# Loads of values, queries and first weights that wait for the start of a page of TensorE's program

## The chip, the cores and the metric

The kernel runs on one core of a Trainium2 chip. Its five engines run their own instruction streams: TensorE (PE in the profile; PEld are its weight loads), VectorE (DVE), ScalarE (ACT), GpSimd (POOL) and SyncE (SP). Here SyncE issues nearly all of the transfers between the chip's main memory and the on-chip buffers. The metric is the time of one execution in microseconds (us) of device time. [...]

## What is computed

A block-sparse attention layer feeds a mixture of experts with one expert per token. The attention has 4 batches, 8 heads, 768 positions and 64 values per head; positions are grouped in 24 blocks of 32.

```python
scores = scale * np.matmul(q, k.transpose(0, 1, 3, 2))
# kept: the blocks beside the diagonal, the first and last block of rows and of columns,
# and three sampled blocks for each block of queries; all others are set to -1e9
attn = softmax(scores)
x = np.matmul(attn, v)                      # as 3072 tokens of 512
...
do_compute = x @ w_skip > 0
e_idx = argmax(x @ w_gate)                  # one of 8 experts, 512 -> 1024 -> 512
out[do_compute] = x + gate * (relu(x @ w1[e]) @ w2[e])
```

## The kernel before, in words

The first and the last block of queries attend to all positions. They are worked first, by 16 units of the class `Dense`. The other 22 blocks of queries ("columns") each attend to at most eight blocks of keys: the first, the last, three near ones and three sampled ones. They are worked by 44 units of the class `Sparse`, two for each column, `b = 0` and `b = 2`, that is, two of the four batches each. `ORDER` takes the columns in turn from the lower and from the upper half (1, 12, 2, 13, ...), and each half has one store of keys (`kg`) and one of values (`va`, `vb`), so a store is refilled while the other half's column is worked.

A unit has these steps: `S` (16 score matmuls of PE, L452), `M` (maxima on DVE, L458), `X` (exponentials on ACT, L464), `T` (transposes on PE, L471), `V` (their copy by ACT, L477), `A` (32 matmuls with the values, L490) and `N` (division by the sums on DVE, L501 to L503, into `xs`). `sparse_step(k)` interleaves them by hand: `S` of unit k+2, `N` of unit k-1, `T` of unit k+1, `A` of unit k, then `M` and `X` of unit k+2, then `after` of unit k-1, which issues four stores of the finished column, and `fill`, which issues what is due by step number. In between come small pieces of routing (`work`). The whole program order is fixed when the kernel is built; `manual_schedule` keeps it.

The loads in question are issued by SyncE, in the order of the program:

- `load_v(i)`, called at the end of `A` of a column's second unit, for the next column of the same store. It loads one near block and three sampled blocks, 260 KB each, into the store that this `A` was the last to read. The numbers of the sampled blocks are read into three registers of SyncE between the first load and the others. The next `A` on this store is three units later.
- `load_q(i)`, called in `S` of a column's first unit: 512 KB of queries, for two columns at once, so in every second column. `load_k`, called in `S` of the second unit, has GpSimd copy the blocks of keys within the chip (L204, L223) and then scale the queries.
- `load_w`, called in `fill` in the last steps of the stage, two loads of 512 KB a step: the weights of the first expert, in four quarters each (`"1"`, then `"2"`). They go into `kts`, where the keys were. `split_w` then makes two parts of each piece: ACT writes `w1h` (L545), GpSimd `w1l` (L547).

Near the end of the stage two groups of early tokens are fetched (`xe`, L639) and transposed (L622), and their two parts written by ACT (`xeh`, L624) and DVE (`xel`, L625). Then the experts begin: matmuls from L878 on. `xs` has two buffers, so a column's `N` writes where the second column before it was stored from.

Of the kernel before, what the change touches and what calls it, by code (L numbers as in the profile page):

```python
# [20 lines left out]
NB, BS = 24, 32  # L21
# [3 lines left out]
N, DM, E, FF = 3072, 512, 8, 1024  # L25
# [8 lines left out]
LC = NC + 2  # L34
NEVER = float(E * LC * P * P)
VA = 8
NEAR = 8
KINDS = [1, 2, 4, 5, 6, 8, 9, 10, 11, 12]
HALF = NB // 2

ORDER = [i for pair in zip(range(1, HALF), range(HALF, NB - 1)) for i in pair]
# [5 lines left out]
def tile_kernel(ctx, tc, qs, qd, kt, v, sb, wg, w1, w2, out):  # L47
    nc = tc.nc
# [3 lines left out]
    vrows = v.rearrange("n s b h d -> n s (b h) d")  # L52
# [29 lines left out]
    def load_dense_k(u):  # L82
        b, pp = divmod(u, 4)
        if u == 0:
            qts[b] = dp.tile([P, 4, 64], F32, name="qt", bufs=3)
            nc.sync.dma_start(out=kts[:, 0, 0:384], in_=kt[0, :, 0, 0:384])
            nc.scalar.dma_start(out=qts[b][:, 0], in_=qd[b, :, 0])
            nc.sync.dma_start(out=kts[:, 0, 384:768], in_=kt[0, :, 0, 384:768])
            nc.scalar.dma_start(out=qts[b][:, 1:4], in_=qd[b, :, 1:4])
            return  # L90
        if pp == 0:
            qts[b] = dp.tile([P, 4, 64], F32, name="qt", bufs=3)
            nc.sync.dma_start(out=qts[b], in_=qd[b])
        nc.sync.dma_start(out=kts[:, u], in_=kt[b, :, pp])

    def load_dense_v(u):

        b, pp = divmod(u, 4)
        if u % 2 == 0:
            vts[u] = vts[u + 1] = dp.tile([P, 6, 4, VD], F32, name="vt", bufs=VA // 2)  # L100
        elif u > 1:
# [3 lines left out]

    for u in range(VA):
        load_dense_k(u)
# [92 lines left out]
    def vslot(x, z):  # L200
        return vslots[x][z // 4][z % 4]
# [4 lines left out]
    def store(i):  # L206
        return i // HALF

    def window(i):
        return (i - 1, i, i + 1) if i in ORDER[:2] else (i + 1,)  # L210

    def next_of(i):
        return i + 1 if i + 1 in ORDER and store(i + 1) == store(i) else None
# [16 lines left out]
    qt, qts2 = {}, {}  # L230

    def load_q(i):
        z = ORDER.index(i)
        if z % 2 == 0:
            qts2[z // 2] = ap.tile([P, 2, NPAIR, BS], F32, name="q")
            for n in range(2):
                qt[ORDER[z + n]] = qts2[z // 2][:, n]
            nc.sync.dma_start(out=qts2[z // 2], in_=qs[z // 2])

    def load_v(i):  # L240
        x = store(i)
        if i in ORDER[:2]:
            nc.sync.dma_start(out=vslot(x, 0), in_=vrows[0])
            nc.sync.dma_start(out=vslot(x, 1), in_=vrows[NB - 1])
        for blk in window(i):
            nc.sync.dma_start(out=vslot(x, 4 + blk % 3), in_=vrows[blk if 0 < blk < NB - 1 else NB])
        for vr, z in zip(blocks_of(mybir.EngineType.SP, vidx, i, NB), (2, 3, 7)):
            nc.sync.dma_start(out=vslot(x, z), in_=vrows[bass.ds(vr, 1)].rearrange("n s h d -> (n s) h d"))


    def route(xta, tiles):
# [186 lines left out]
    class Sparse:  # L438
# [6 lines left out]
        def S(self):  # L445
            self.sp = [ps_s.tile([P, 2, 256], F32, name=f"sp{w}") for w in range(2)]
            for g in range(2):
                for a in range(4):
                    p = 4 * (self.b + g) + a
                    for w in range(2):  # L450
                        ws = slice(64 * w, 64 * w + 64)
                        nc.tensor.matmul(out=self.sp[w][32 * a:32 * a + 32, g], lhsT=qt[self.i][ws, p, :], rhs=kg[self.x][ws, p, :].rearrange("p (k c j) -> p c k j", k=2, j=2), start=True, stop=True)  # L452
            if next_of(self.i):
                (load_k if self.b else load_q)(next_of(self.i))

        def M(self):
# [22 lines left out]
        def A(self):  # L479
            drain = self.i == NB - 2 and self.b == 2  # L480
            if drain:
                self.op = ps_s.tile([P, 512], F32, name="sp0")[:, 0:4 * VD].rearrange("p (g w d) -> p g w d", g=2, w=2)
            else:
                self.op = ps_o.tile([P, 2, 2, VD], F32, name="op")
            for g in range(2):
                for w in range(2):
                    for t in range(2):
                        vt = (va, vb)[t][self.x]
                        for a in range(4):
                            nc.tensor.matmul(out=self.op[32 * a:32 * a + 32, g, w, :], lhsT=self.pt[:, g, 2 * w + t, 32 * a:32 * a + 32],  # L490
                                             rhs=vt[:, 8 * (self.b + g) + 2 * a + w, :], start=(t == 0), stop=(t == 1))
            if self.b == 2 and next_of(self.i):
                load_v(next_of(self.i))

# [33 lines left out]
    raws = {}  # L528

    perm = rt.tile([1, E], I32, name="perm")  # L530
# [3 lines left out]
    def load_w(which, p, part=0, parts=1, place=None, er=None):  # L534

        n = 4096 * ((2 * p - (which == "1")) % 3 if place is None else place)
        raws[which, p] = kts.rearrange("p a s -> p (a s)")[:, n:n + 4096]
        sz = 4096 // parts
        cs = slice(sz * part, sz * part + sz)
        er = nc.sync.value_load(perm[0:1, p:p + 1], min_val=0, max_val=E - 1) if er is None else er  # L540
        nc.sync.dma_start(out=raws[which, p][:, cs], in_=(w1 if which == "1" else w2)[bass.ds(er, 1), :, cs].rearrange("o p c -> (o p) c"))

    def split(h, l, r, what, eng=None):
        if "h" in what:
# [130 lines left out]
    def mix(a, c):  # L675
        n = max(len(a), len(c))
        for z in range(n):
            for l in (a, c):
                if z < len(l):
                    l[z]()  # L680
# [37 lines left out]
    def fill(q):  # L718

        if q == 1:  # L720
            first.extend(setup())
        if 1 <= q <= 7:
            mix(first[4 * q - 4:4 * q], [])
        if 0 <= q and q + VA < 18:
            if q + VA < 16:
                load_dense_k(q + VA)
            load_dense_v(q + VA - 2)
        if q in (8, 10):
            i = ORDER[q // 2 - 4]
            load_q(i)  # L730
            load_v(i)
            load_k(i)
        if q == nd:
            den.close()
            wp = ctx.enter_context(tc.tile_pool(name="wp", bufs=1, side="right"))
            wt.update({"1" + t: wp.tile([P, 4096], F32R, name=f"w1{t}") for t in "hl"})
        z = q - nq + 10
        if -4 <= z < 4:
            load_w("12"[(z + 4) // 4], 0, z % 4, 4)
        if 3 <= z < 11:  # L740
            split_w("1", 0, z - 3, 8, "hl", nc.gpsimd)

# [106 lines left out]
    now = mc.tile([1, 2 * E], I32, name="now")  # L849
# [146 lines left out]
    def parts(p):  # L996

        def each(f):
            if NEAR <= f + 3 < NK2:
                split_w("1", p, f + 3, 8)  # L1000
# [155 lines left out]
    x = [mp.tile([P, NK1, CS * P], F32R, name=n, bufs=1) for n in ("xh", "xl")]  # L1156
# [114 lines left out]
```

## Time and profile before

| what | value |
| --- | --- |
| median of 3 runs | 491.8 us (489.98 to 494.74) |
| profiled execution | 492.82 us |
| its span, first to last instruction | 491.1 us |
| instructions in the span | 16939 |
| PE busy | 441.3 us |
| DVE busy | 321.2 us |
| ACT busy | 250.8 us |
| POOL busy | 149.3 us |
| granted clock of TensorE, mean | 0.97 |

The profile comes from one execution, and its times count from the first instruction. "Busy" is the time in which an engine works on an instruction; a matmul of 32-bit numbers is run as two passes, each with its own weight load. "Idle before" is the time in which an engine did nothing ahead of an instruction, with what ended it: another engine's instruction, a DMA, or "issue", where the profile shows no semaphore that it waited for. The DMA share is the mean busy share of 16 DMA engines.

### The profile page before, as it was taken

What the parts mean: (1) busy time and instruction counts of PE and PEld (TensorE: products, weight loads), DVE (VectorE), ACT (ScalarE), POOL (GpSimd) and SP (SyncE); (2) the same over time, 40 slices, a digit from 0 to 9 for tenths busy, and PEclk for the clock granted to TensorE, in tenths of its full rate; (3) what the DMA queues carried; (4) which work ended last, traced back from release to release, by engine and by line L of the source; (5) the groups of instructions that cost most, each with busy time, mean ns of one, the idle gap of its engine ahead of it and who ended that gap; (6) DMA issues with size and microseconds to landing.
All of it is one profiled execution on the core that took longest, in us unless ns stands there. A gap on an engine that the chain in (4) does not pass through costs nothing. (4 is left out here: it accounts for less than half of the span.)

```text
span 491.1 us, 16939 instructions
## 1 busy us (share of the span) xinstructions
PE 441.3 (90%) x6666; PEld 342.1 (70%) x6666; DVE 321.2 (65%) x838; ACT 250.8 (51%) x581; POOL 149.3 (30%) x198
## 2 busy tenths in 40 slices
PE   5989999889999999997499999899999894999994
PEld 1757777666667666655477789787878664878984
DVE  2878766956878776956565286664777776465621
ACT  2535586756766765667231264463435484343500
POOL 2004625433443433426604420403313142201002
PEclk9989999999999999999689999999999995999999
DMA  8998837765767765779328209383371949281001
GB/s 253 375 301 282 306 117 222 244 206 160 241 187 238 214 186 177 235 230 332 102 94 311 92 27 332 107 294 112 109 274 53 337 148 328 82 301 38 23 16 45
DMA packets 43824, 94.91 MB, mean 193 GB/s; under 512 B 7463, under 2 KB 27048, under 8 KB 40546
## 3 DMA queue, kind: packets, MB, share of 16 engines
q1 hardware_dynamic: 39808, 84.27, 51.8%
q0 software_dynamic: 3376, 8.09, 4.7%
q8 instruction: 74, 1.21, 1.0%
q14 instruction: 132, 1.08, 0.7%
q10 hardware_dynamic: 434, 0.26, 0.2%
HBM read 84.51 MB, written 10.88 MB: 194 GB/s over the span
## 5 line engine op out<-in xcount | busy, mean ns | idle before, releaser
L477 ACT COPY pt<-tp 128x512 f32<-128x512 f32 x88 | 52.3, 598 | 48.2 <-PE tp L471 48.2
L464 ACT ACTIVATE pr<-sp,m 128x256 f32<-128x256 f32 x176 | 69.0, 482 | 3.5 <-DVE m L458 3.2
L458 DVE TENSOR_REDUCE m<-sp 128x2 f32<-128x512 f32 x88 | 56.5, 684 | 18.5 <-PE sp L452 18.2
L878 PE MATMUL hp<-xh,w1h 128*128 128x256 f32 (+3 forms) x192 | 57.8, 301 | 2.5 <-PE yp L934 2.5
L880 PE MATMUL hp<-xh,w1l 128*128 128x256 f32 (+3 forms) x192 | 57.4, 299 | 0.0
L879 PE MATMUL hp<-xl,w1h 128*128 128x256 f32 (+3 forms) x192 | 57.4, 299 | 0.0
L883 ACT ACTIVATE hh<-hp 128x256 fp32r<-128x256 f32 (+2 forms) x56 | 21.3, 380 | 68.5 <-PE hp L880 53.3
L452 PE MATMUL sp<-kg,q 64*32 64x256 f32 x1408 | 53.9, 391 | 2.6 <-issue 2.4
L490 PE MATMUL op<-va,pt 128*32 128x65 f32 x1376 | 46.2, 223 | 6.5 <-issue 5.6
L471 PEld LDWEIGHTS tp<-ident,pr 128*128 128x128 f32 x352 | 37.6, 141 | 20.4 <-issue 7.4
L204 POOL COPY kg<-kts 128x512 f32<-128x512 f32 x30 | 19.4, 663 | 105.9 <-PE sp L452 68.6
L74 POOL DMA_INDIRECT out<-o,lt x17 | 17.0, 998 | 112.5 <-DVE o L949 107.6
L932 PE MATMUL yp<-w2h,hh 128*128 128x512 f32 x120 | 49.1, 409 | 1.9 <-DVE o L949 1.9
L471 PE MATMUL tp<-ident,pr 128*128 128x128 f32 x352 | 48.8, 280 | 0.8 <-ACT pt L477 0.7
L933 PE MATMUL yp<-w2l,hh 128*128 128x512 f32 x120 | 48.1, 400 | 0.3 <-issue 0.3
L934 PE MATMUL yp<-w2h,hl 128*128 128x512 f32 x120 | 47.8, 398 | 0.0
L547 DVE TENSOR_TENSOR w2l<-kts,w2h 128x512 fp32r<-128x512 f32 x64 | 43.5, 686 | 5.7 <-ACT w2h L545 3.3
L490 PE MATMUL op<-vb,pt 128*32 128x65 f32 x1376 | 44.3, 220 | 1.8 <-issue 1.7
L223 POOL COPY kg<-kts 128x512 f32 x66 | 42.1, 684 | 8.1 <-POOL kg L204 8.1
L490 PEld LDWEIGHTS op<-va,pt 128*32 128x32 f32 x1376 | 32.7, 109 | 15.3 <-issue 13.8
L886 DVE SCALAR_TENSOR_TENSOR hl<-hp,hh 128x256 fp32r<-128x256 f32 (+2 forms) x56 | 23.4, 417 | 30.3 <-ACT hf L885 12.7
L545 ACT CAST w2h<-kts 128x512 fp32r<-128x512 f32 x64 | 39.0, 619 | 1.8 <-DVE w1l L547 1.8
(221 smaller groups left out, 902.2 us busy)
## 6 DMA issues: line engine op xcount, KB each, us to landing
kts<-w SPq DMA_DIRECT2D x64, 512.0 KB, 6.3
va<-v SPq DMA_DIRECT2D x48, 260.0 KB, 3.9
vb<-v SPq DMA_DIRECT2D x48, 260.0 KB, 4.2
kts<-kt SPq DMA_DIRECT2D x15, 384.0 KB, 7.5
q<-qs SPq DMA_DIRECT2D x11, 512.0 KB, 5.4
out<-xs SPq DMA_DIRECT2D x88, 64.0 KB, 4.2
vt<-v SPq DMA_DIRECT2D x7, 780.0 KB, 8.7
vt<-v SPq DMA_DIRECT2D x2, 390.0 KB
```

The source lines that it names most:

```text
L452: nc.tensor.matmul(out=self.sp[w][32 * a:32 * a + 32, g], lhsT=qt[self.i][ws, p, :], rhs=kg[self.x][ws, p, :].rearrange("p (k c j) -> p c ...
L458: return [lambda w=w: nc.vector.tensor_reduce(out=self.mx[:, w], in_=self.sp[w], axis=AX.X, op=ALU.max, negate=True) for w in range(2)]
L464: nc.scalar.activation(out=self.pr[:, g, w], in_=self.sp[w][:, g], func=AF.Exp, bias=self.mx[:, w, g:g + 1])
L471: nc.tensor.transpose(out=tp[:, u, :], in_=self.pr[:, g, u // 2, (u % 2) * P:(u % 2) * P + P], identity=ident)
L477: nc.scalar.copy(out=self.pt[:, g], in_=self.tp[g])
L490: nc.tensor.matmul(out=self.op[32 * a:32 * a + 32, g, w, :], lhsT=self.pt[:, g, 2 * w + t, 32 * a:32 * a + 32], rhs=vt[:, 8 * (self.b + g) ...
L878: nc.tensor.matmul(out=hp[:, 0:w], lhsT=wh[:, f, k, :], rhs=xh[:, k, 0:w], start=(k == 0), stop=False)
L879: nc.tensor.matmul(out=hp[:, 0:w], lhsT=wh[:, f, k, :], rhs=xl[:, k, 0:w], start=False, stop=False)
L880: nc.tensor.matmul(out=hp[:, 0:w], lhsT=wl[:, f, k, :], rhs=xh[:, k, 0:w], start=False, stop=(k == NK1 - 1))
L932: nc.tensor.matmul(out=yp, lhsT=hh[:, f, cs], rhs=wh[:, f, :], start=(f == 0), stop=False)
L933: nc.tensor.matmul(out=yp, lhsT=hh[:, f, cs], rhs=wl[:, f, :], start=False, stop=False)
L934: nc.tensor.matmul(out=yp, lhsT=hl[:, f, cs], rhs=wh[:, f, :], start=False, stop=(f == NK2 - 1))
```

## The change

The kernel estimates, while it is built, how many instructions TensorE has run, and so where each page of 256 instructions begins. `size_of` counts a matmul as four instructions, a transpose as two; the term `done // 149` stands for others, and `PROLOGUE` for those ahead of the kernel. Loads of the three kinds are no longer issued where they are called: `paged` puts them on a list, sorted by size (260 for values, 512 for queries and weights). `page_check`, called in `S` and `A`, sees when a new page has begun and has `release` issue the smallest loads, up to 1600 KB together, each with a dependency on the instruction of TensorE that began the page. `release()` without an argument issues all that are left, without such a dependency; this is done in `S` of a column's second unit, ahead of `load_k`, and once in `fill`, at the step where the last two weight loads were issued. The loads for the first two columns stay as they were. The eight weight loads are put on the list together, at the step of the first of them, and share one register for the expert's number. The registers of the sampled blocks are still read in `load_v`.

```diff
+PAGE = 256
+PROLOGUE = 98
...
-            nc.sync.dma_start(out=qts2[z // 2], in_=qs[z // 2])
+            load = lambda: nc.sync.dma_start(out=qts2[z // 2], in_=qs[z // 2])
+            load() if i in ORDER[:2] else paged(512, load)
...
+    class Paged:
+        waiting, seen, done, page = [], 0, 0, None
+
+    def size_of(i):
+        if type(i) is mybir.InstLdweights:
+            return 1
+        if type(i) is mybir.InstMatmult:
+            return 1 if i.ldweights is False else 2 if i.is_transpose else 4
+        return 0
+
+    def paged(size, load):
+        Paged.waiting.append((size, load))
+        Paged.waiting.sort(key=lambda w: w[0])
+
+    def release(most=1 << 30, ins=None):
+        while Paged.waiting and most >= Paged.waiting[0][0]:
+            size, load = Paged.waiting.pop(0)
+            most -= size
+            dma = load()
+            if ins is not None:
+                tc.add_manual_dep(dma.ins, ins.name, mybir.DependencyInfo(mybir.DependencyClass.Sync, mybir.DependencyReason.DATA),
+                                  reason="behind the fetch of a page")
+
+    def page_check():
+        bb = nc.cur_bb.bb.instructions
+        for i in bb[Paged.seen:]:
+            Paged.done += size_of(i)
+            page = (Paged.done + Paged.done // 149 + PROLOGUE) // PAGE
+            if page != Paged.page and size_of(i):
+                Paged.page = page
+                release(1600, i)
+        Paged.seen = len(bb)
...
+        now = (lambda size, load: load()) if i in ORDER[:2] else paged
         for blk in window(i):
-            nc.sync.dma_start(out=vslot(x, 4 + blk % 3), in_=vrows[blk if 0 < blk < NB - 1 else NB])
+            now(260, lambda blk=blk: nc.sync.dma_start(out=vslot(x, 4 + blk % 3), in_=vrows[blk if 0 < blk < NB - 1 else NB]))
         for vr, z in zip(blocks_of(mybir.EngineType.SP, vidx, i, NB), (2, 3, 7)):
-            nc.sync.dma_start(out=vslot(x, z), in_=vrows[bass.ds(vr, 1)].rearrange("n s h d -> (n s) h d"))
+            now(260, lambda vr=vr, z=z: nc.sync.dma_start(out=vslot(x, z), in_=vrows[bass.ds(vr, 1)].rearrange("n s h d -> (n s) h d")))
...
+                    page_check()
             if next_of(self.i):
+                if self.b:
+                    release()
                 (load_k if self.b else load_q)(next_of(self.i))
...
+                        page_check()
...
-        if -4 <= z < 4:
-            load_w("12"[(z + 4) // 4], 0, z % 4, 4)
+        if z == -4:
+            er = nc.sync.value_load(perm[0:1, 0:1], min_val=0, max_val=E - 1)
+            for n in range(8):
+                paged(512, lambda n=n: load_w("12"[n // 4], 0, n % 4, 4, er=er))
+        if z == 3:
+            release()
```

## Rows read from the trace of the kernel before

**Rows 1.** Busy time of PE, and the queue of instructions, on the page.

```profile
PE 441.3 (90%) x6666; PEld 342.1 (70%) x6666; DVE 321.2 (65%) x838; ACT 250.8 (51%) x581; POOL 149.3 (30%) x198
...
q8 instruction: 74, 1.21, 1.0%
```

**Rows 2.** Windows: busy (count) of PE, PEld, DVE, ACT, POOL; clock, DMA share, GB/s.

```profile
61.40:86.00 24.60, 24.40 (x707) 17.47 (x708) 16.13 (x43) 18.43 (x44) 9.74 (x15) 1.00 0.55 169
86.00:110.00 24.00, 20.86 (x641) 15.03 (x639) 17.54 (x53) 15.21 (x38) 9.89 (x14) 1.00 0.73 224
```

**Rows 3.** Waits of PE from 61 to 211: total us, times, longest.

```profile
PE op L490 <- issue: 6.1, 8, 1.3
PE sp L452 <- issue: 2.4, 4, 0.8
```

**Rows 4.** Timeline of PE, three resumptions: start, us, what, idle before.

```profile
153.76 0.26 PE L490 MATMUL op<-va,pt 128*32 128x65 f32 x3 [0.57 <-issue]
...
176.86 0.25 PE L490 MATMUL op<-va,pt 128*32 128x65 f32 x2 [1.19 <-issue]
...
210.09 0.42 PE L342 MATMUL rps<-phi,lsb 128*128 128x48 f32 x2 [1.19 <-issue]
```

**Rows 5.** Windows of two pages, columns as in rows 2.

```profile
171.82:176.86 5.04, 3.85 (x128) 2.83 (x128) 3.72 (x15) 3.18 (x9) 2.27 (x4) 1.00 0.61 185
...
158.07:162.12 4.05, 4.05 (x127) 2.60 (x133) 2.39 (x8) 2.65 (x7) 2.35 (x4) 1.00 0.60 180
```

**Rows 6.** DMA at 174.4:174.5, 177.9:178.0, 155.2:155.3: packets, MB, share.

```profile
q8 instruction: 1, 0.02, 58.2%
...
q8 instruction: 1, 0.02, 65.5%
...
q8 instruction: 1, 0.02, 69.1%
```

**Rows 7.** Timeline of SyncE, value loads: start, us, issues.

```profile
154.23 0.49 SPq L246 DMA_DIRECT2D vb<-v  x1
155.63 1.14 SPq L248 DMA_DIRECT2D va<-v  x2
...
169.96 1.16 SPq L248 DMA_DIRECT2D va<-v  x2
```

**Rows 8.** Window from the start to a resumption, columns as in rows 2.

```profile
0.00:93.87 93.87, 84.75 (x1600) 58.68 (x1601) 65.22 (x216) 53.14 (x119) 29.04 (x60) 0.98 0.80 265
```

**Rows 9.** Instructions of L490, its events: ns min/median/max, first and last.

```profile
L490 PEldq EVENT_SEMAPHORE  x85: 51/51/747, 63.4 to 229.8; - x85
```

**Rows 10.** DMA issues from 61 to 232: count, KB each, median us to landing.

```profile
vb<-v SPq DMA_DIRECT2D x40, 260.0 KB, 4.2
...
q<-qs SPq DMA_DIRECT2D x9, 512.0 KB, 5.4
kts<-w SPq DMA_DIRECT2D x8, 512.0 KB, 6.3
```

**Rows 11.** Timeline of PE, first values used of one column.

```profile
164.25 0.32 PE L490 MATMUL op<-va,pt 128*32 128x65 f32 x8
```

**Rows 12.** Timeline of SyncE, last columns and weights.

```profile
220.46 0.51 SPq L246 DMA_DIRECT2D vb<-v  x1
...
226.46 3.28 SPq L511 DMA_DIRECT2D out<-xs  x4
```

**Rows 13.** Timelines of PE, DVE and POOL, last columns.

```profile
229.48 0.32 PE L490 MATMUL op<-va,pt 128*32 128x65 f32 x8 [0.91 <-DMA va<-v]
...
233.65 0.42 DVE L503 TENSOR_TENSOR xs<-op,rs 128x256 f32<-128x256 f32 x1 [2.30 <-DMA out<-xs]
...
235.53 0.66 PE L622 MATMUL rps<-ident,xe 128*128 128x128 f32 x4 [2.98 <-DVE xel L625]
...
228.37 6.21 POOL L547 TENSOR_TENSOR w1l<-kts,w1h 128x512 fp32r<-128x512 f32 x5 [3.52 <-ACT w1h L545]
```

**Rows 14.** Window of the half clock, columns as in rows 2.

```profile
236.00:249.80 13.80, 9.38 (x41) 7.04 (x40) 5.94 (x12) 3.56 (x8) 6.06 (x9) 0.51 0.14 34
```

More of the change, by code (lines that the diff above doesn't have):

```diff
@@ L540, in load_w @@
         er = nc.sync.value_load(perm[0:1, p:p + 1], min_val=0, max_val=E - 1) if er is None else er
-        nc.sync.dma_start(out=raws[which, p][:, cs], in_=(w1 if which == "1" else w2)[bass.ds(er, 1), :, cs].rearrange("o p c -> (o p) c"))
+        return nc.sync.dma_start(out=raws[which, p][:, cs], in_=(w1 if which == "1" else w2)[bass.ds(er, 1), :, cs].rearrange("o p c -> (o p) c"))
     def split(h, l, r, what, eng=None):
```

## The prediction

> **What bounds it now.** I read the busy times first: TensorE (PE) is busy 441.3 us, 90% of the span, and the queue of instructions, q8, brings 74 packets of together 1.21 MB, so 16 KB each [rows 1]. The change touches the sparse stage, from about 61 to 235 us, so I then read windows there. Between 61.4 and 86 PE is busy 24.4 of 24.6 us; between 86 and 110 only 20.9 of 24, while VectorE (DVE) is at 17.5 and GpSimd at 9.9 [rows 2]. PE sets the pace, and what keeps it from work is to be looked for in its waits.
>
> From 61 to 211 us they have one cause, "issue", which is no semaphore and no engine: 6.1 us before L490, 2.4 before L452 [rows 3] and 1.2 before L342 [rows 4], 9.7 us in 13 waits, none over 1.3. The timeline shows what they look like: PE stops in the middle of a run of equal matmuls and goes on with the same line, as at 153.76, 176.86 and 210.09 [rows 4]. Between two such resumptions, 171.82 and 176.86, lie 128 matmuls and 128 weight loads [rows 5]: 256 instructions, and 16 KB over 256 is 64 bytes each, so PE waits for a page of its own code.
>
> The packets show why. The page entered at 171.82, the resumption before, calls for the next; that packet starts between 174.4 and 174.5, 2.6 us later, takes 58.2% of 16 x 0.1 = 0.9 us, and PE goes on at 176.86, 1.4 us behind its end. The page entered at 176.86 has its packet just after 177.9, 1.1 us later [rows 6]. So
>
> stop = (entry to packet) + 1.0 + 1.4 - length of the page.
>
> With 1.1 that is a fetch of 3.5 us; a page that isn't stopped lasts 4.05 [rows 5], so there is about half a microsecond to spare for queueing. What stood in the queue at 171.82: the value loads issued from 169.96 to 171.1 [rows 7] among others; at 176.86 these were long down.
>
> **The loads go behind the fetch.** The mark in `page_check` must hit the right instruction. Up to the resumption at 93.87 the trace has 1600 + 1601 instructions of PE [rows 8]; 3201 + 3201 // 149 + 98 = 3320, 8 short of 13 x 256, a tenth of a microsecond, and the few bf16 matmuls of the ranks, which `size_of` counts as four where two run, close that. So the marks fit the program before. The new dependencies add signals to some 30 TensorE instructions. If each cost an event instruction of its own it would be 30 x 51 ns = 1.5 us [rows 9] and the marks would drift; I take 0, since a matmul can carry a signal (the bound is 1.5).
>
> The nearest row to a load behind the entry is the page entered at 153.76 [rows 4], with the first load issued at 154.23 [rows 7]: the packet that it called came just after 155.2 [rows 6], 1.5 us behind the entry, so 1.5 + 2.4 = 3.9 us, and PE has no stop before the page entered at 158.07 [rows 5], 4.3 us on. So the page in which a column's loads go out costs nothing. The page after it meets the tail: four loads of 260 KB, every second column 512 KB of queries, and four stores, which are not marked. The values of a column need 4 x 0.57 us to issue (two in 1.14 [rows 7]) and 4.2 to land [rows 10], so they are down some 6 us after the release; the next call comes after about 4.1, waits perhaps a microsecond, and its page just hides that. With queries there is one more issue, and 5.4 us to land [rows 10]: I put 0.4 us of stop on each of the 9 query loads, 3.6, with a rest about 4 us. So of 9.7 us I take 5.7 as gained. Bounds: 9.7 if no tail is met, 0 if each stop only moves one page on.
>
> [...]
>
> **The values come later.** The wait holds a column's loads by up to a page: those free at 154.23 [rows 7] wait for the page entered at 158.07 [rows 5], 3.8 us, and the mean is half a page, 2.1. Their user, the column's first `A`, starts at 164.25 [rows 11]. With 0.3 us for the signal, 3 x 0.57 to the last issue and 4.2 to land, these end at 164.3, just at the edge; the mean case ends 1.7 us early. Two things help: the register loads that now part the first load from the second (154.23 to 155.63 [rows 7]) are done ahead of the wait, and `release()` in `S` of the column's second unit bounds the delay. Since PE without stops gets to `A` sooner, I charge 0.1 us for some 5 of 20 columns near that edge, 0.5. Bounds: 0, and the slower rival below.
>
> **Queries, stores, scaling.** Queries are asked for two columns ahead, so a page and 5.4 us are hidden by the units between. GpSimd scales them behind its key copies and has room (9.9 of 24 us busy [rows 2]); were that cover gone, `S` would wait. Behind the waiting load on SyncE stand the stores of the finished column; their buffer is written again two columns later, so a page of delay costs nothing. I charge 0.
>
> **The last columns and the first weights.** Now SyncE issues two weight loads of 512 KB a step, and they hold back what follows: the last column's values go out from 220.46, and the stores of the column before from 226.46, with two more weight loads in between [rows 12]. The values stop PE 0.9 us at 229.48; for the stores DVE waits 2.3 us at 233.65, and through it PE 2.98 us at 235.53, with the second transpose of the early rows; then ScalarE, then GpSimd's last splits [rows 13]. After the change one weight load goes out with the values of column 11 at the page of 210.1 [rows 4], three at the next (a page is 4.1 us: 214.2), and at the one after, 218.3, the last column's values with the fifth weight load behind them. The last three go behind the stores. So the values leave 2 us and the stores some 4 us earlier: the 0.9 vanishes, and the transpose can follow its unit and the first `xel` at about 232.9, 2.6 us sooner. Then GpSimd's splits bound it: five took 6.21 us from 228.37 [rows 13], two more at that rate end at 237.1, where PE was still idle. I take 2.9 in all; bounds 0 and 0.9 + 3.0 = 3.9. The clock is at half level, 0.51, from 236 to 249.8, behind these idle times, with 9.4 us of PE's work in it [rows 14]. PE still idles for GpSimd and at the branch, so I leave that; if the clock stayed up, up to half of the 9.4 would be won, and this is why the low end is below the sum.
>
> **Sum.** The profiled execution took 492.8 us, its span 491.1 and 1.7 around it. 492.8 - 5.7 - 2.9 + 0.5 = 484.7. The median of the runs is 1.0 below the profiled one, which gives 483.7: forecast 484.
>
> **Rivals.**
> - All stops go: 492.8 - 9.7 - 2.9 - 1.0 = 479. For it: without the register loads a burst is shorter. Against: queries and stores in its tail. 0.14.
> - The stops move one page on, as the bytes are the same: some 8.5 of 9.7 us stay, 492.8 - 1.2 - 2.9 + 0.5 - 1.0 = 488. For it: DMA is busy 0.73 of the window that has the worst stops [rows 2]. 0.13.
> [...]
> - It doesn't do what it says: the marks drift off the pages, loads wait for nothing useful, and stops stay: 490 to 491. 0.05.
> - Slower: the values land too late for `A`. If the released bursts landed in the 6.3 us of the weight loads [rows 10] in place of 4.2, the column of 164.25 would be 2.2 us late and the mean one 0.4; at 0.8 for 20 columns that is 16 us: 492.8 + 16 - 8.6 - 1.0 = 499. It decides from 5.9 us to land onwards, where the mean case's margin of 1.7 is used up. 0.09.
>
> My forecast has 0.50, with 481 to 487 as its own range. Faster by over 1% (under 486.9) takes most of that, the first rival and the edge of the second: 0.62. Within 1%, about what runs from 489.98 to 494.74 can tell from no change: 0.29. Slower 0.09. The range from 478 to 491.5 takes in all but the slower rival and the far edge of the first.
>
> **What would show it.** Right: between 61 and 205 us PE's "issue" falls from 9.7 to about 4; the q8 packet of a page that releases loads starts 1.1 to 1.8 us behind its entry; L490 waits for values under 1 us in all; weights are issued in threes, and DVE's wait for the stores at its last `xs` is gone. Wrong: "issue" stays near 9 with its stops a page later, or L490 waits for `va` or `vb` in many columns, or PE has stops of 2 us and the clock falls within the stage.

## The result, and the profile after

The changed kernel took 497.37 us (median of 4 runs, 495.66 to 499.75), the kernel before 492.06 in the same comparison (489.98 to 494.74): a ratio of 1.0143, with an interval of 1.0095 to 1.0191. The forecast was 484.0, so even its sign was wrong. The profiled execution is the run of 495.66 us, its span 493.9. Ratios, and the times given beside them, rest on undisturbed runs alone; two profiles were taken in disturbed ones (the marks half a page off, and values and stores both behind marks), and they are read for what is waited for, not to the microsecond.

The page has the same work as [rows 1]: as many instructions of every engine, PE busy about as long, and as many packets of code.

```profile
PE 440.0 (89%) x6666; PEld 344.7 (70%) x6666; DVE 319.4 (65%) x838; ACT 251.8 (51%) x581; POOL 147.7 (30%) x198
...
q8 instruction: 74, 1.21, 1.0%
```

To see where the time went I cut both executions at three places: the first attention product `A` of a sparse unit, the 41st (the last but three), and the first matmul `hp` of an expert. Windows of the kernel after (columns as in rows 2):

```profile
63.20:223.55 160.35, 144.72 (x4298) 102.93 (x4297) 116.33 (x357) 105.97 (x253) 59.36 (x88) 0.98 0.64 192
223.55:245.44 21.89, 11.88 (x317) 9.46 (x317) 13.51 (x41) 11.60 (x25) 13.25 (x13) 0.83 0.86 295
245.44:493.90 248.46, 227.93 (x1328) 193.20 (x1328) 145.75 (x288) 103.75 (x241) 57.78 (x57) 0.96 0.44 155
```

and the same three of the kernel before:

```profile
64.68:220.28 155.60, 145.36 (x4298) 102.59 (x4297) 117.30 (x357) 105.54 (x253) 60.08 (x89) 1.00 0.67 204
220.28:240.22 19.94, 10.20 (x317) 7.48 (x317) 13.43 (x41) 11.29 (x25) 12.32 (x11) 0.90 0.83 278
240.22:491.10 250.88, 228.85 (x1328) 193.48 (x1328) 146.80 (x289) 103.60 (x241) 59.79 (x59) 0.96 0.44 153
```

The counts of PE agree, so these are equal stretches of work. The stage is 4.75 us longer (160.35 - 155.60); PE isn't busier in it, so its idle time rose, from 10.2 us (155.60 - 145.36) to 15.6. The last columns are 1.95 longer where 2.9 less were forecast. The part ahead of the stage (64.68 to 63.20) is 1.5 shorter and the experts are 2.4 shorter. Together that is +2.8, the difference of the two profiled executions (495.66 - 492.82).

Waits of PE from 61 to 211 us after the change, to be read beside [rows 3] (L532 is L490 of before, `A`; L491 is L452, `S`; L513 is L471, the transposes):

```profile
PE op L532 <- DMA vb<-v: 9.0, 8, 2.2
PE op L532 <- DMA va<-v: 2.7, 3, 1.6
PE op L532 <- DMA out<-xs: 2.0, 1, 2.0
PE op L532 <- issue: 1.0, 1, 1.0
PE tp L513 <- ACT pt L519: 0.9, 3, 0.4
```

What to see here is a swap. "Issue", the stops at pages of code, fell from 9.7 to 1.0 us, further than forecast; and `A`, which waited for no values before, waits 13.7 us for them (9.0 + 2.7 + 2.0; the wait put down to a store ended at 192.49, just behind the last signal of a load of values, at 192.35).

That "issue" means a page can be checked by counting. In the kernel before, all 13 of these waits end at places a multiple of 256 instructions of PE apart (matmuls, weight loads and those of its sequencer), to within one instruction. A matmul of 32-bit numbers counts there as it runs: the 1408 matmuls of `A` (44 units of 32) are 2816 in the trace, with 2816 weight loads; the 352 transposes of `T` are 352, and the 17 bf16 matmuls of the ranks at L291 are 17. From 61 to 236 us there are 37 places of such a count and 37 packets of q8 (36 and 36 after the change), so these are taken for PE's code. By this count the beginnings of pages are given below, also where PE doesn't stop at them.

One of these waits, in the timeline of PE and SyncE (start, length, what; idle before):

```profile
97.93 0.33 PE L532 MATMUL op<-vb,pt 128*32 128x65 f32 x7
...
102.69 0.50 SPq L285 DMA_DIRECT2D vb<-v  x1
103.38 2.24 SPq L287 DMA_DIRECT2D va<-v  x2
...
105.80 0.47 SPq L287 DMA_DIRECT2D vb<-v  x1
...
106.99 1.81 SPq L554 DMA_DIRECT2D out<-xs  x4
...
108.34 0.32 PE L532 MATMUL op<-va,pt 128*32 128x65 f32 x8 [0.21 <-DMA va<-v]
109.94 0.50 SPq L285 DMA_DIRECT2D vb<-v  x1
...
110.85 0.32 PE L532 MATMUL op<-vb,pt 128*32 128x65 f32 x8 [2.19 <-DMA vb<-v]
```

The last product on a store ends at 98.25 and its successor on the same store begins at 108.34, 10.1 us later. In between the four loads must go out and land. They went out 4.4 us behind that end, for the page was entered at 102.37; the fourth was issued 3.1 us behind the first; the last signal of its landing came 5.0 us later, at 110.81, and PE had stood still for 2.4 us. The next group shows the other way of being late: its store was free at 105.90, a page began at 106.04, but in SyncE's order the loads stand behind the four stores of 106.99 and go out at 109.94.

Over all 20 groups, worked out in the same manner, the first load goes out 3.5 us on the mean behind the end of the product (1.05 to 6.36; 0.06 in the median before the change), the last signal of a landing comes 5.8 to 8.6 us behind the first issue in 19 of them (9.8 in the last), and from product to product on one store there are 8.3 to 14.2 us.

DVE waits too, 5.8 us between 61 and 211 (none before), for stores of finished columns that stand behind loads that wait for a mark; PE doesn't wait for DVE there.

Three of PE's waits in the stage are of 2 us and more. Behind two of them, not behind the one that ends at 78.50, the clock fell. Windows of PE after the change (length, busy, granted clock, DMA share, GB/s); in the kernel before both stretches are at 1.00:

```profile
111.00:115.50 4.50, 4.50 (x98) 0.62 0.92 299
192.00:197.00 5.00, 4.51 (x96) 0.67 0.91 284
```

### The profile page after: what moved, and what is told of

The parts are those of the page before. It is cut to its first block, busy times and chain, and to the rows that moved or that the text cites. A ratio compares the mean times of both kernels' runs of the same rounds, so it can differ in the third digit from the quotient of the medians.

```text
span 493.9 us, 16920 instructions
## 1 busy us (share of the span) xinstructions
PE 440.0 (89%) x6666; PEld 344.7 (70%) x6666; DVE 319.4 (65%) x838; ACT 251.8 (51%) x581; POOL 147.7 (30%) x198
## 5 line engine op out<-in xcount | busy, mean ns | idle before, releaser
L532 PE MATMUL op<-vb,pt 128*32 128x65 f32 x1376 | 44.5, 223 | 15.5 <-DMA vb<-v 9.0
L930 ACT ACTIVATE hh<-hp 128x256 fp32r<-128x256 f32 (+2 forms) x56 | 21.3, 381 | 67.8 <-PE hp L927 63.4
L513 PEld LDWEIGHTS tp<-ident,pr 128*128 128x128 f32 x352 | 38.8, 144 | 21.2 <-ACT pr L506 8.2
L491 PE MATMUL sp<-kg,q 64*32 64x256 f32 x1408 | 51.9, 401 | 0.0
L513 PE MATMUL tp<-ident,pr 128*128 128x128 f32 x352 | 50.2, 286 | 0.9 <-ACT pt L519 0.9
L532 PE MATMUL op<-va,pt 128*32 128x65 f32 x1376 | 45.7, 225 | 3.7 <-DMA va<-v 3.6
L532 PEld LDWEIGHTS op<-vb,pt 128*32 128x32 f32 x1376 | 34.3, 111 | 17.6 <-issue 9.6
L532 PEld LDWEIGHTS op<-va,pt 128*32 128x32 f32 x1376 | 33.1, 111 | 10.5 <-issue 5.4
```

The costliest lines, as they stand in the source:

```text
L513: nc.tensor.transpose(out=tp[:, u, :], in_=self.pr[:, g, u // 2, (u % 2) * P:(u % 2) * P + P], identity=ident)
```

## The experiments

They are told in four steps. Where the values are wrong, routing and expert work differ, so such a kernel is compared with others of the same wrong values. One profile's stage is good to about 2 us: before the change it is 155.6 us, and in three variants that issue the values just as it does 154.0, 154.9 and 156.3 (below).

### Which of the marked loads costs it

In the first kernel weights alone wait; the second has only the change of the last two lines, so queries and weights wait.

```diff
-            load() if i in ORDER[:2] else paged(512, load)
+            load()
-        now = (lambda size, load: load()) if i in ORDER[:2] else paged
+        now = lambda size, load: load()
```

Weights alone. 

> The kernel after the change, in which values and queries are issued at once, as before the change, and only the first expert's weights wait for a mark. Theory (the values cost it): the stage is that of the kernel before, with 8 to 11 us of page stops and at most 1 us of waits for values, and the time is 489 to 493 us. Rival (the tail and the weights cost it): the stage is that of before, and the time is 495 us or more.

Ratio 1.0056 [0.9984, 1.0127], 494.23 us. Stage 154.0 us, 8.2 us of "issue" from 61 to 211, no wait for values. In the last columns, though, `A` waits 3.0 us for `va`, and from the 41st product to `hp` there are 21.4 us for 19.9 before: the weights go out earlier in threes, and the last values stand behind them.

Queries and weights. 

> The kernel after the change, in which the values are issued at once, as before the change, and the queries and the first expert's weights wait for marks. Theory (the values cost it, and the queries have room to wait): no waits for values over 1 us in sum between 61 and 211 us, page stops of 7 to 10 us, since the queries are one transfer in nine of the stage, and the time is 488 to 492 us, faster than the kernel before by at most 0.5%. Rival (queries behind a mark hold up the scores or the tail): waits for queries of over 1 us at the transposes, or 494 us and more.

Ratio 1.0032 [0.9950, 1.0115], 491.48 us; stage 154.9, issue 9.6, no wait for values, and 21.3 us of last columns. Neither kernel can be told from the one before.

The third marks values and nothing else.

```diff
-            load() if i in ORDER[:2] else paged(512, load)
+            load()
...
-        if z == -4:
-            er = nc.sync.value_load(perm[0:1, 0:1], min_val=0, max_val=E - 1)
-            for n in range(8):
-                paged(512, lambda n=n: load_w("12"[n // 4], 0, n % 4, 4, er=er))
-        if z == 3:
-            release()
+        if -4 <= z < 4:
+            load_w("12"[(z + 4) // 4], 0, z % 4, 4)
```

> Only the values wait for marks; queries and weights are issued where they were before. Theory (the values are what comes too late): waits of L532's line for values from 61 to 211 stay at 10 us or more, and the time is 494 to 499. Rival (the loss comes from queries and weights, which fill the queue ahead of values or at the end of the stage): waits for values under 4 us and 487 to 492.

Ratio 1.0163 [1.0042, 1.0284], 495.23 us. From 61 to 211 us `A` waits 4.6 us for values (4.1 here, 0.5 for `va`); what is named issue, 3.8 us in all, stands at beginnings of pages:

```profile
PE op L532 <- DMA vb<-v: 4.1, 5, 2.0
PE op L532 <- issue: 3.5, 6, 0.6
```

Stage 158.4 us, last columns 21.5. Neither forecast of the waits came true, 10 us or more or under 4; what decides is the time, since of the three this kernel alone is shown to be slower than the one before. So the marks of the values are enough for a loss, and those of queries and weights by themselves aren't shown to cost anything. Why the waits for values are 4.6 us here and 13.7 with all three marked stays open.

### Is it their lateness

The same marks, half a page away from where pages begin:

```diff
-PROLOGUE = 98
+PROLOGUE = 98 + 128
```

> The changed kernel with PROLOGUE 98 + 128, so that every mark is half a page late. The loads wait as long on average. Theory (it matters that the fetch is called ahead of the loads): the call for the next page comes 2 us behind the first load and meets the burst; issue from 61 to 215 goes back to 6 us or more while the waits for values stay at 12 to 16, so 500 to 505. Rival (only that the loads wait and go in one piece matters, or the longer pages): as the change, 495 to 499, issue under 2 us.

Ratio 1.0250 [1.0145, 1.0355], 503.20 us. PE's waits from 61 to 211:

```profile
PE sp L491 <- issue: 6.2, 6, 2.1
PE op L532 <- issue: 3.6, 7, 1.2
PE op L532 <- DMA vb<-v: 3.4, 4, 1.5
PE op L532 <- DMA va<-v: 3.3, 4, 2.4
```

Both costs stand side by side: the stops of before, 10.2 us, and waits for values of 6.7 us, where the theory had 12 to 16.

Then the values are let go earlier: what still waits goes out in the score products of either unit, not the second alone.

```diff
-                if self.b:
-                    release()
+                release()
```

> The kernel after the change, in which what still waits for a mark is let go in the score products of both units of a batch instead of the second alone, so that values are held back by at most half a batch, about 1.2 us by the even groups of the trace. Theory (the values come too late for the next product on their store): TensorE's waits for values between 61 and 211 us fall from 14 us to under 3 us, some of the page stops come back (3 to 7 us of the 9.7 us), and the time is 487 to 493 us. Rival (the values are not what costs; the loss is in the tail or in the clock): waits for values fall, and the time stays at 495 us or more.

Ratio 1.0017 [0.9955, 1.0078], 492.06 us. From 61 to 211 (`A` is L531 here):

```profile
PE op L531 <- issue: 6.3, 9, 1.8
PE sp L491 <- issue: 3.8, 4, 1.9
```

No wait for values is left, the stops are back in full, 10.1 us, and the time is that of the kernel before. The theory had this right but for the stops, of which it expected 3 to 7 us. So lateness makes the waits. (Of the 5.3 us between this time and that of the changed kernel its one profile has 2.0 in the stage, 158.4 us, and 3.4 in the last columns, 18.5 for 21.9.) But the swap is now nearly exact: whoever lets the values go in time has the stops again. Do marks take the stops away at all, or were these only hidden while PE stood waiting for values, with the fetch running on beside it?

### What the marks are worth when nobody waits for values

In these kernels the loads of values behind the first two columns all write one store, and every product reads the other: the traffic is that of the real kernel, and no product waits for it.

```diff
-        x = store(i)
+        x = store(i) if i in ORDER[:2] else 1
...
-                        vt = (va, vb)[t][self.x]
+                        vt = (va, vb)[t][0]
```

The kernel before with this edit, as a control. 

> The kernel before with the same edit: value loads go at once, into the second store, and every A reads the first. Left out: the values of all columns but the first two are not used. It is the control of the run with marks. Theory: PE waited for values only 0.9 us here, so the time stays within 2 us of the kernel before, with 8 to 11 us of issue between 61 and 211. Rival (the wait of the loads for A, not the place in the page, made the stops): issue falls under 5 us and the time to 487 or less.

Its stage (columns as in rows 2):

```profile
65.23:223.22 157.99, 145.48 (x4297) 103.25 (x4297) 116.78 (x357) 106.07 (x253) 60.09 (x88) 0.99 0.70 208
```

and PE's stops from 61 to 205:

```profile
PE op L490 <- issue: 9.3, 7, 2.8
...
PE sp L452 <- issue: 0.3, 1, 0.3
```

The stops are as forecast, so the rival fell. The whole kernel takes 0.9575 [0.9506, 0.9644] of the kernel before, not within 2 us of it: with wrong values the work behind the stage is another.

The kernel after with the edit. 

> The changed kernel, but every marked value load writes the second store, and every A reads the first, so that no matmul waits for a marked load and no load waits for A. Left out: the values of all columns but the first two are not used. The traffic, its order and the marks stay. Theory (the marks do free the pages; what is lost is 14.7 us of waits for values and the clock behind them): PE's issue waits from 61 to 211 us stay under 2 us, and the time is 497.4 - 14.7 - 3 = 479 to 483. Rival (the page stops vanished only because PE, waiting for values, made its pages longer): with the waits gone the stops come back, 6 to 9 us of issue, and the time is 486 to 490.

Stage 158.3, issue 9.4, ratio 0.9717 [0.9644, 0.9789]. (The 14.7 us hold the 1.0 us of issue as well; the waits for values are 13.7.) This says less than it seems: with fewer event instructions on PE (195 for 224) the counted marks slid ahead of the true beginnings of pages, by some 40 instructions at the end of the stage, and loads went out before the call. So the count was fitted again (within some 7 instructions over the stage):

```diff
-PROLOGUE = 98
+PROLOGUE = 107
...
-            page = (Paged.done + Paged.done // 149 + PROLOGUE) // PAGE
+            page = (Paged.done + Paged.done // 600 + PROLOGUE) // PAGE
```

> The kernel after the change, in which every load of values after the first two batches writes the one store and every attention product reads the other, so that no product waits for values; the marks are counted anew to fall within some six instructions of the page starts. The values are wrong for most blocks, which changes the routing and the expert work behind, so only the stage is compared, with the kernel before under the same edit. Theory (the marks free the pages, and the late values cost what is gained): TensorE's waits named issue come to under 2 us between 61 and 205 us, and from the first attention product to the 41st passes 148 to 150 us, against 158.0 us in the kernel before with the same edit, whose page stops are 9.6 us. Rival (the gain of the pages is only moved, to other instructions or to the next page): at least 6 us of issue, or as long a stage, 156 to 159 us.

```profile
64.39:223.19 158.80, 144.35 (x4298) 101.90 (x4297) 116.85 (x356) 106.17 (x253) 58.66 (x88) 1.00 0.66 197
```

and PE's stops from 61 to 205:

```profile
PE op L532 <- issue: 3.1, 5, 1.1
PE sp L491 <- issue: 2.8, 3, 1.9
PE op L532 <- DVE xs L546: 1.8, 2, 1.6
PE tp L513 <- issue: 1.6, 1, 1.6
```

The rival held. Issue is 7.5 us (9.8 over the whole stage, 10.7 in the control), the stage as long as in the control, and the whole kernel 0.9654 [0.9572, 0.9736], no faster than the control. Marks that hit make the stage no shorter, though no product waits for values. They do hold something back: the stores stand behind the waiting loads, DVE waits 12.2 us for them (0.4 in the control), and PE 1.8 of that.

How much was there to win? The kernel before without the loads of values:

```diff
+        if i not in ORDER[:2]:
+            return
         for blk in window(i):
```

> The kernel before the change, without the four loads of values of each block after the first two: the products read what the first two blocks left, so the values are wrong, the routing and the expert work behind differ, and only the stage is compared. It bounds what any order of the values' loads can be worth to the pages. Theory (values' loads are one part of what stands ahead of the fetches of pages, the stores of the results the other): the waits named issue between 61 and 205 us fall from 9.4 us in the kernel before with the same wrong values to 3 to 6 us, and the first to the 41st product takes 151 to 155 us against 158.0 us. Rival (it is the values' loads alone): under 1.5 us of issue and under 150 us.

```profile
62.11:205.49 143.38, 141.14 (x4298) 101.00 (x4297) 117.10 (x356) 106.11 (x253) 59.97 (x89) 1.00 0.32 86
```

and PE's stops from 61 to 205:

```profile
PE op L492 <- issue: 0.9, 2, 0.5
```

The rival again: without these loads the stops are gone, though the stores stay (0.9 us left, 2.2 us of idle time in all), and the stage is 14.6 us shorter. (The products read other wrong values than in the control, but the stage has the same count of matmuls.) The gain that the prediction aimed at exists; the order of the loads doesn't fetch it.

### Why marked loads still hold up pages

Either because some loads were let go without a mark and stores were never marked, or because a load behind one page's beginning still stands ahead of the next page's call. First every load of values is kept until a mark comes, and queries are issued at once (the fitted count and the edit by which nobody waits stay, and aren't shown again):

```diff
-                if self.b:
-                    release()
```

> As the run with marks that fit in which nobody waits for values, but no load of values is let go without a mark: each stands behind the beginning of a page, however late. Queries are issued at once. The values are wrong, so only the stage is compared, with 158.0 us from the first product to the 41st and 9.7 us of page stops between 61 and 205 us in the kernel before under the same edit, 158.8 and 9.2 us in the run with marks that fit, and 143.4 and 0.9 us without any loads of values. Theory (the loads that were let go without a mark, and the stores, still stand ahead of the fetches): issue falls to 3 to 6 us and the stage to 149 to 155 us, since the stores still go unmarked. Rival (a marked load fills the queues so long that the fetch of the next page comes behind it all the same): issue of 7 us or more and 156 us or more.

```profile
64.74:220.32 155.58, 144.22 (x4297) 102.12 (x4297) 114.70 (x356) 106.05 (x253) 59.03 (x88) 1.00 0.68 201
```

and PE's stops from 61 to 205:

```profile
PE op L530 <- issue: 4.3, 7, 1.1
PE sp L491 <- issue: 1.6, 2, 1.0
...
PE tp L511 <- issue: 0.8, 1, 0.8
```

(By the waits shown above the stops are 9.6 us in the control and 7.5 in the run with marks that fit; 9.2 is the count to 211 us.) Issue is 6.7 us, a little under the rival's 7, and the stage 155.6, at its lower edge: between the two, with the whole at 0.9675 [0.9634, 0.9715]. The edit does less than was meant. Counted in the program as it is built, all 80 loads of values stood behind marks already, in the changed kernel and in the run with marks that fit; there the call without a mark let go queries and weights alone. So only the queries differ between this run and that one, and both show stops with every load of values behind a mark. The timeline of one page shows how (start, length, what; idle before):

```profile
118.12 0.26 PE L530 MATMUL op<-vb,pt 128*32 128x65 f32 x3 [0.23 <-issue]
...
118.46 0.50 SPq L285 DMA_DIRECT2D vb<-v  x1
119.16 2.50 SPq L287 DMA_DIRECT2D va<-v  x2
121.85 0.48 SPq L287 DMA_DIRECT2D vb<-v  x1
122.43 1.99 SPq L552 DMA_DIRECT2D out<-xs  x4
...
122.58 0.26 PE L530 MATMUL op<-va,pt 128*32 128x65 f32 x3 [0.69 <-issue]
...
127.29 0.25 PE L530 MATMUL op<-va,pt 128*32 128x65 f32 x2 [0.83 <-issue]
```

and the DMA of 124.8 to 124.9 (packets, MB, share of 16 engines):

```profile
q8 instruction: 1, 0.02, 77.1%
```

The loads begin 0.34 us behind the page entered at 118.12, as meant. The fourth goes out at 121.85; the last signals of the third and the fourth come at 124.22 and 125.52. The next page is entered at 122.58, in the middle of this, and its call for a packet is served between 124.8 and 124.9, 2.2 us later; PE runs out of code and resumes at 127.29, 0.83 us late. From first issue to last landing the four loads take 7.1 us, longer than a page. The stores of 122.43 stand there as well; that they don't make the stops by themselves is seen in the run without the loads of values (0.9 us of stops). No run spread the four loads over several pages, which would vary the length of the burst alone.

Then the stores are marked as well, up to the 18th block (`(...)` stands for the store as it was):

```diff
+            held = (lambda size, load: load()) if i in ORDER[18:] else paged
             for hh in range(4):
-                nc.sync.dma_start(...)
+                held(261, lambda hh=hh: nc.sync.dma_start(...))
...
-                release(1600, i)
+                release(2400, i)
```

> As the run in which all values stand behind marks, with the stores of results, up to the 18th block, behind marks as well: but for one load of queries in two blocks nothing of the stage is issued but just behind the beginning of a page. Theory: issue of at most 3 us between 61 and 205 us, and 146 to 151 us from the first product to the 41st. Rival (the transfers of a page run on to the beginning of the next): 6 us or more and 155 us or more.

Ratio 0.9884 [0.9810, 0.9959], slower than without marked stores; the stage of its profile is 173.4 us. PE's waits from 61 to 236:

```profile
PE op L530 <- DVE xs L544: 11.4, 3, 5.1
PE op L530 <- issue: 8.5, 6, 2.7
PE sp L491 <- issue: 1.4, 2, 1.1
```

With next to everything of the stage behind marks the stops are there still, 9.9 us, and the stores come so late that DVE, which fills their buffer anew, holds PE. The rival held.

Two versions were tried in search of a gain. Stores marked in place of values, up to the 15th block (the store's lines as above, values at once as in the first diff):

> The kernel after the change, in which the values are issued at once, as before the change, and the four stores of each block's results wait for marks in their place, up to the 15th block; queries and weights wait as in the change. Nobody needs a store for more than a block's time, so holding it back makes nothing late. Theory (pages are held up by whichever transfers stand ahead of the fetch; only work with room can wait): no waits for values, the waits named issue between 61 and 211 us fall from 9.7 to 4 to 7 us, and the time is 486 to 491 us. Rival (every transfer moved off one page's fetch lands on the next one's): issue stays at 8 us or more and the time at 490 to 495 us.

Ratio 1.0003 [0.9936, 1.0069]; no wait for values in the stage, issue 10.1 us from 61 to 211, stage 156.3. The rival's issue, and no gain. But it tests little: counted in the program, 16 of the 60 stores went out by a mark and 44 by the call without one. Values held half a batch at most, and stores marked (`only` limits what is let go to loads of that size):

```diff
-                if self.b:
-                    release()
+                release(only=None if self.b else 260)
```

> The kernel after the change, in which values wait for a mark or at most until the next score products, as in the run that released them in every product, and the stores wait for a mark too, up to the 15th block. Theory (as for the run with the stores alone): waits for values under 2 us and issue 3 to 7 us between 61 and 211 us, and 486 to 491 us, no better than with the stores alone, since most values are let go ahead of their mark. Rival: issue of 8 us or more and 490 to 495 us.

Ratio 0.9961 [0.9917, 1.0006] over ten runs, 489.42 us; waits for values 2.0 us, issue 8.2, stage 159.2. It is not shown to be faster than the kernel before, and no version here is.

## Why the prediction was wrong

Two steps failed. The larger is "The values come later": a term of 0.5 us that measured 13.7. The other is "The loads go behind the fetch", whose gain is there only while PE waits for values.

**What bounds it.** Right: PE's idle time in the stage is made by pages, and pages by the loads of values (0.9 us of stops without these, 9.6 in the control with them).

**The loads go behind the fetch.** This step failed, 5.7 us of forecast gain. Right in it: marks hit within some ten instructions, the new signals cost no event instruction (224 as before), and loads with nothing ahead of them on SyncE go out 0.3 to 0.4 us behind the entry. In the pages that release values the packet starts 0.3 to 2.6 us behind the entry, 5.9 once; the sign named was 1.1 to 1.8. It failed where it said that the values "are down some 6 us after the release; the next call comes after about 4.1, waits perhaps a microsecond, and its page just hides that". The loads land 5.8 to 8.6 us after the release, and the pages of the kernel before last 3.4 to 5.8 us, so the next call stands behind them: 2.2 us in the page above, where the prediction's formula has room for 1.6 (1.1 and the half microsecond to spare). Measured by itself, the mean from entry to packet over the 31 to 34 pages between 61 and 205 us (every 256th instruction of PE and the q8 packets, paired in order) is 1.8 us in the control, 1.7 with marks that fit, 1.8 with every value behind a mark, and 0.9 without the loads. The second rival, that stops move one page on, was right for the pages.

That the changed kernel's own stops fell to 1.0 us speaks against this only at first sight: its PE waits 13.7 us for values, in 12 waits, and a packet of q8 runs during 8 of them. How much that hid can be estimated from the traces, page by page. PE would stop by the end of the next page's packet, plus 1.38 us to resume (the mean of the 13 stops before the change), less the time at which the page would have ended without its waits. Over the pages entered between 61 and 206 us the stops come to 10.0 us for the kernel before, where 9.7 were measured, 9.2 (9.2) with marks that fit and 8.9 (8.8) with every value behind a mark; for the changed kernel to 6.6, where 1.0 was measured. So of the 8.7 us that went some 5.5 were hidden by the waits. Some 3 were won by calls that were served earlier: the mean from entry to packet in the changed kernel is 1.4 us, 1.9 before. This is an estimate, not a run; the runs without waits for values, in which 6.7 to 7.5 us of stops stay, point the same way.

**The values come later.** The term was 0.5 us and measured 13.7 us of waits. Right was the price of the landing (the DMA issues of the kernel after give a median of 4.0 us for `vb`, 4.2 in [rows 10]). Wrong were three sizes. The deferral, taken as half a page, 2.1 us, is 3.5 on the mean: loads that find a store free just behind a mark wait for a whole page, and others stand behind four stores in SyncE's order. From the first issue to the fourth there are 2.0 to 3.1 us, 2.5 on the mean, and not 3 x 0.57 = 1.7; the row with two issues in 1.14 us has them 0.66 apart. And the room was read off one product: from the end of one to the next on its store there are 8.3 to 14.2 us, and 3.5 + 2.5 + 4.2 = 10.2 is more than the shorter of these. `release()` in the second unit, named as what bounds the delay, let go no load of values at all. Letting them go half a batch earlier (48 of the 80 then go without a mark) took all these waits away, and the changed kernel's loss with them.

The slower rival, 499 us for 497.4 measured, was right in its mechanism and wrong in its cause: it asked for a landing slower than before, and the landing stayed as it was. It put 16 us on the waits, which is near the 13.7 measured, and kept its gains of 8.6 us beside them. In the stage the stops did fall by 8.7, for the most part under cover of the waits, so 13.7 - 8.7 = 5.0 of loss, for 4.75 by the windows. That its time comes near the measured one is luck in part: 2.9 of its gains were put on the last columns, which lost 1.95.

**Queries, stores, scaling.** Charged 0, and right for the queries (with queries and weights marked there is no wait at the scores). For stores "a page of delay costs nothing" held for PE in the changed kernel, where DVE waits 5.8 us for them and PE not for DVE; delayed longer, with the stores marked too, they cost PE 11.4 us of waits.

**The last columns.** Forecast 2.9 us of gain, measured 1.95 of loss. Waits of PE from 211 to 250 after the change:

```profile
PE hp L925 <- DVE xta L561: 5.1, 1, 5.1
PE op L532 <- issue: 2.8, 1, 2.8
PE op L532 <- DMA va<-v: 1.0, 1, 1.0
...
PE rps L665 <- DVE xel L668: 0.4, 1, 0.4
```

The wait that the term was built on did go: 3.0 us before the second transpose became 0.4 ([rows 13]). What it freed was taken by a stop at a page (2.8, at 230.70, none before), by late values, and by a longer wait at the first expert matmul (4.0 before). The 0.9 us for the last column's values didn't vanish: these went out at 225.64, 4.9 us behind their store's release, not 2 us earlier, behind stores and three weight loads. With weights alone marked the stretch is 21.4 us, with values alone 21.5, so either is enough for the loss. In the two versions that have all the marks but let values go after half a batch it is 18.5 and 17.8 us, one profile each: some of the forecast gain is there when the last values aren't late.

## What to carry to other kernels

Before transfers are moved behind a short critical one, compare how long their burst occupies the queues with the time to the next critical one: here the four loads took 7.1 us in the page shown, and pages last 3.4 to 5.8; with marks that hit, 7.5 us of stops stayed where the control has 9.6. Price a deferral by its worst alignment and against the shortest gap between last use and next use of the buffer, over all iterations, and not by a mean and one row. And when one kind of wait disappears while another appears, take the second away in a run before crediting the first.

## What was not expected of the hardware

- Without the loads of values not only idle time fell. For the same counts of matmuls PE's busy time is 141.1 us for 145.5 in the control, so some 4 us of what is counted as busy comes with the transfers. The granted clock isn't the cause: the kernel before has 145.4 us at 1.00, as the run without the loads has. What it is stays open.
- Two waits of 2.0 and 2.2 us within the stage, in which PE is busy 90% of the time, were followed by stretches in which the granted clock was 0.62 and 0.67 on the mean, with 0.50 from 111.8 to 115.1 and from 193.7 to 197.0 us; a third wait of 2.1 us wasn't. The prediction had named this as a sign of being wrong. What it cost isn't shown: PE's busy time in the stage is 144.7 us, 145.4 before.
